# Attention and gated MLP on one core: the first K, Q and V units placed later, their K evictions shared by tokens

## The chip, the core and the metric

The kernel runs on one core of a Trainium2 chip. The core has a matrix engine (TensorE; PE in the profile, with its weight loads as PEld), a vector engine (VectorE, DVE), an activation engine (ScalarE, ACT), a general engine (GpSimd, POOL) and a queue engine (SyncE, SP). Each works through its own instructions in order and waits on semaphores for the others. The metric is the time of one execution on the device, in microseconds; lower is better.

## The reference

x has 2048 tokens of 512 features, all tensors are bfloat16. The result is the sum of three terms:

```
xn  = layernorm(x)
A   = sliding-window attention of xn: 32 heads of 16, causal, window 256; its output @ wo
z   = gelu(x @ w_in)                    # 2048 x 1376, split in z1 and z2, 688 each
z2  = layernorm(z2)
g   = w_sp @ z2 + b_sp                  # w_sp mixes tokens, 2048 x 2048
B   = (z1 * g) @ w_out
out = x + A(xn) + B(xn)
```

Both branches take xn: B's `x` is the normalized x.

## The kernel before

Tokens are cut into 16 blocks of 128. The program has two stages, and the order of every engine's instructions is that of the source (a manual schedule).

**Stage one** (lines 235 to 452) makes everything that needs whole rows first. x arrives by DMA in pairs of blocks. DVE takes mean and variance (`stat_steps`, L316 and L317), blocks 0 to 3 get their root from ACT (`root`, L361) and DVE's reciprocal (`norm_root`, L367), later blocks from a chain of twelve small DVE operations (`rsqrt_steps`, L112 to L129), and `norm_apply` (L321) normalizes in place. `transpose_x` turns a block on PE (L330) and ACT copies it to `xnT` (L333). A *z half* is eight matmuls, one block by one half of w_in (`do_z`, L342); ACT's `gelu` (L358) evicts it to `z1_all` or `z2_all`. z halves have three PSUM buffers. The halves come in a fixed order: both halves of blocks 0 to 8 (`Z_BOTH` is 9), then the second halves of 9 to 15, then the first halves of 9 to 15. `z2_steps` (L208, L214) are DVE's statistics of z2 for its layernorm; one block takes two readings and one aggregation; `z2_norm` (L221) applies them at the end of the stage, for all 16 blocks.

Between z halves stand nine *early units*, the projections that the second stage needs first: K and Q of tokens 0 to 511 for each of four head groups, and V of block 0, in the order K0, Q0, K1, Q1, K2, Q2, K3, Q3, V0 (list `early`). A unit is four matmuls of 512 columns (`unit_k` L157, `unit_q` L176, `unit_v` L191). Their PSUM tiles (`me`) come from the two buffers that the transposes (`tp`) and the first zero matmuls (`wm`) use too, in turn, so a unit waits until the tile two before it has been evicted. A K unit is evicted twice, each time multiplied by one of two head masks (`emask`, e = 0 and 1), into `k_ring`, whose last axes are mask and token: L169 on DVE for e = 0, and for early units L167 on ACT for e = 1. Q is evicted by ACT (L184), V by DVE in four casts of 64 x 256 (L203).

What DVE does around these, in its order: normalization of the last x blocks, `clear_strips` of five attention tiles (ten memsets, L97 and L100), two memsets of ones into `v_ring` (L405), which five transfers of zeros (L270) have filled before, then from block 5 on z2 statistics and evictions in turn. Fourteen matmuls of zeros (L287) keep PE busy while x arrives.

**Stage two** (from line 454) is the attention and the rest of the MLP. 128 gaps `t` each have one `quad` (scores S, L549, exponentials by ACT, L559), masks by DVE (L575), and in between work picked by a budget: further K, Q and V units (PSUM tile `m`, three buffers, tag "w", shared with `gf`), the token mixing `gf` (L473, 512 matmuls, evicted by L479), attention times V (`o_t`, L590) and the outputs (L507, L515). PE's first rows there are S, V1, four gf, S, a Q unit, four gf, S, a second Q unit. V1 is evicted by DVE (L203).

Of the kernel before, what the change touches and what calls it, by code (L numbers as in the profile page):

```python
# [12 lines left out]
ACT = mybir.ActivationFunctionType  # L13
ALU = mybir.AluOpType
# [4 lines left out]
DH = 16  # L19
# [13 lines left out]
HK = 64  # L33
# [5 lines left out]
Z_BOTH = 9  # L39
# [5 lines left out]
def kernel(  # L45
# [12 lines left out]
    nc = tc.nc  # L58
# [13 lines left out]
    k_ring = pers.tile([P, NG, 2 * QRING, 2, HK], BF, name="k_ring")  # L72
    v_ring = pers.tile([P, VRING, 2, H // 2, 2, DH + 1], BF, name="v_ring")
# [3 lines left out]
    emask = pers.tile([P, 2], F32, name="emask")  # L77
# [16 lines left out]
    e_bufs = [ep0.tile([P, 8 * EPAD + HK], BF, name=f"E{i}") for i in range(E_EARLY)]  # L94

    def clear_strips(eb):
        nc.vector.memset(  # L97
            eb[:, 0 : 8 * EPAD].rearrange("p (j c) -> p j c", c=EPAD)[:, :, 0:HK], 0.0
        )
        nc.vector.memset(eb[:, 8 * EPAD : 8 * EPAD + HK], 0.0)  # L100
# [35 lines left out]
    def weave(a, b):  # L136
        for i in range(max(len(a), len(b))):
            if i < len(a):
                a[i]()
            if i < len(b):  # L140
                b[i]()
# [4 lines left out]
    def m_tile(tail=False, early=False):  # L146
        if early:
            return early_pool[0].tile([P, 512], F32, name="me", tag="t")[:]
        if tail:
            t = ps_s.tile([P, 2, 512], F32, name="mt", tag="S")  # L150
            return t[:, 0, :]
        return ps_w.tile([P, 512], F32, name="m", tag="w")[:]

    def unit_k(G, grp, on_act=False, early=False):
        m = m_tile(early=early)
        for c in range(NDC):
            nc.tensor.matmul(  # L157
                m, lhsT=wqkv[:, c, D + G * P : D + (G + 1) * P],
                rhs=xnT[:, 4 * grp : 4 * grp + 4, c, :],
                start=(c == 0), stop=(c == NDC - 1),  # L160
            )
        o = (grp % 2) * 8
        m = m.rearrange("p (a k) -> p a k", k=HK)
        for e in range(2):
            dst = k_ring[:, G, o : o + 8, e, :]
            if on_act and e == 1:
                nc.scalar.activation(out=dst, in_=m, func=ACT.Copy, scale=emask[:, e : e + 1])  # L167
            else:
                nc.vector.tensor_scalar(  # L169
                    out=dst, in0=m, scalar1=emask[:, e : e + 1], scalar2=None, op0=ALU.mult  # L170
                )

    def unit_q(G, grp, on_act=False, early=False):
        m = m_tile(early=early)
# [30 lines left out]
    def z2_steps(n):  # L205
        st = sml.tile([P, 2, nc.vector.BN_STATS_DIM], F32, name="st2")
        steps = [
            lambda j=j: nc.vector.bn_stats(  # L208
                out=st[:, j, :], in_=z2_all[:, n, j * 344 : (j + 1) * 344]
            )  # L210
            for j in range(2)
        ]
        steps.append(
            lambda: nc.vector.bn_aggr(  # L214
                out=mv2[:, n, :], in_=st[:].rearrange("p a b -> p (a b)")
            )
        )
        return steps
# [16 lines left out]
    with tc.tile_pool(name="win_pool", bufs=1) as winp, tc.tile_pool(  # L235
# [8 lines left out]
        nc.vector.memset(esel[:], 1.0)  # L244
        nc.vector.memset(eps_t[:], LN_EPS)
        nc.vector.memset(w_out_sb[:, NFC - 1, :], 0.0)
        early_pool.append(ps_t)
        xs_tiles = {}
        for n2 in range(NB // 2):
# [6 lines left out]
            else:  # L256
                nc.sync.dma_start(
                    out=xs[:],
                    in_=x2[2 * n2 * P : (2 * n2 + 2) * P, :].rearrange("(j p) d -> p j d", p=P),
                )  # L260
            if n2 == 1:
                for c in range(3):
                    (nc.scalar if c < 2 else nc.sync).dma_start(
                        out=w_in_sb[:, c, :], in_=B_w_in[c * P : (c + 1) * P, :]
# [4 lines left out]
        for k in range(VRING):  # L269
            nc.sync.dma_start(  # L270
                out=v_ring[:, k].rearrange("p a g e d -> p (a g e d)").rearrange(
                    "p (r c) -> p r c", c=544
                ),
                in_=warm[:].unsqueeze(1).to_broadcast([P, 2, 544]),
# [5 lines left out]
            out=w_out_sb[:, 0:5, :], in_=B_w_out[0:640, :].rearrange("(c p) n -> p c n", p=P)  # L280
# [2 lines left out]

        make_identity(nc, ident[:])
        wm = ps_t.tile([P, 512], F32, name="wm", tag="t")
        for i in range(14):
            nc.tensor.matmul(wm[:], lhsT=warm[:, 0:P], rhs=warm[:, 0:512], start=True, stop=True)  # L287

        for e in range(2):
            pe = slice(e * HK, (e + 1) * HK)  # L290
            nc.gpsimd.affine_select(
                out=mask2[pe, 0, :], in_=mask2[pe, 0, :], pattern=[[1, HK]],
# [3 lines left out]
                out=mask2[pe, 1, :], in_=mask2[pe, 1, :], pattern=[[-1, HK]],  # L296
# [3 lines left out]
            out=esel[:], in_=esel[:], pattern=[[-32, 4]], compare_op=ALU.is_ge,  # L300
# [3 lines left out]
            out=esel[:], in_=esel[:], pattern=[[32, 4]], compare_op=ALU.is_ge,  # L304
# [7 lines left out]
        def stat_steps(lo, hi):  # L312
            steps = []
            for n in range(lo, hi):
                st = sml.tile([P, nc.vector.BN_STATS_DIM], F32, name="st", bufs=6)
                steps.append(lambda n=n, st=st: nc.vector.bn_stats(out=st[:], in_=xs_tiles[n]))  # L316
                steps.append(lambda n=n, st=st: nc.vector.bn_aggr(out=mvx[:, n, :], in_=st[:]))  # L317
            return steps

        def norm_apply(n):  # L320
            nc.vector.tensor_scalar(  # L321
                out=xs_tiles[n], in0=xs_tiles[n], scalar1=mvx[:, n, 0:1],
                scalar2=rstdx[:, n : n + 1], op0=ALU.subtract, op1=ALU.mult,
            )

        def transpose_x(n):
            tp = ps_t.tile([P, NDC, P], BF, name="tp", tag="t")
            xn = xs_tiles.pop(n)
            for c in range(NDC):
                nc.tensor.transpose(  # L330
                    out=tp[:, c, :], in_=xn[:, c * P : (c + 1) * P], identity=ident[:]
                )
            nc.scalar.copy(out=xnT[:, n], in_=tp[:])  # L333
# [16 lines left out]
        def do_z(n, half):  # L350
            zp = z_tile()
            for c in range(NDC):
                z_part(zp, n, half, c)
            return zp

        def gelu(n, half, zp):
            dst = z1_all if half == 0 else z2_all
            nc.scalar.activation(out=dst[:, n, :], in_=zp[:, 0:FH], func=ACT.Gelu_apprx_tanh)  # L358

        def root(n):  # L360
            nc.scalar.activation(  # L361
                out=rstdx[:, n : n + 1], in_=mvx[:, n, 1:2], func=ACT.Sqrt, bias=eps_t[:],
                scale=1.0,
            )

        def norm_root(n):
            nc.vector.reciprocal(out=rstdx[:, n : n + 1], in_=rstdx[:, n : n + 1])  # L367
            norm_apply(n)
# [5 lines left out]
        root(1)  # L374
        norm_root(0)
        transpose_x(0)
        weave(stat_steps(2, 3), [])
        root(2)
        norm_root(1)
        transpose_x(1)  # L380
        weave(stat_steps(3, 4), [])
        root(3)
        norm_root(2)
# [4 lines left out]
        for lo, hi, nxt in ((4, 8, 8), (8, 12, 14), (12, NB, NB)):  # L388
# [4 lines left out]
            if lo == 4:  # L393
                nc.vector.tensor_reduce(
                    out=emask[:, 0:1], in_=esel[:], op=ALU.add, axis=mybir.AxisListType.X
                )
                nc.vector.tensor_scalar(
                    out=emask[:, 1:2], in0=emask[:, 0:1], scalar1=-1.0, scalar2=1.0,
                    op0=ALU.mult, op1=ALU.add,
                )  # L400
                nc.vector.tensor_copy(out=b_all[:], in_=b_bf[:])
        for eb in e_bufs:
            clear_strips(eb)
        for e in range(2):
            nc.vector.memset(v_ring[e * HK : (e + 1) * HK, :, :, :, e, DH : DH + 1], 1.0)  # L405

        early = [(unit_k, 0), (unit_q, 0), (unit_k, 1), (unit_q, 1), (unit_k, 2), (unit_q, 2),
                 (unit_k, 3), (unit_q, 3), (unit_v, 0)]
        stats_done = 0
# [11 lines left out]
        order = [(1, 1)] + [(n, h) for n in range(2, Z_BOTH) for h in range(2)]  # L421
# [3 lines left out]
        for i, (n, half) in enumerate(order):  # L425
            zp = do_z(n, half)
            if next_t < NB and (half == 0 or n >= Z_BOTH or n == 1):
                transpose_x(next_t)
                next_t += 1
            gelu(n, half, zp)  # L430
            if n >= 6 and (half == 1 or i >= len(order) - 2) and early:
                u, a = early.pop(0)
                if u is unit_v:
                    u(a, early=True)
                else:
                    u(a, 0, on_act=True, early=True)
            if n >= 5:
                ready = n if half == 1 or n < Z_BOTH else NB
                for _ in range(1 if half == 0 and n < Z_BOTH else 2):
                    if stats_done == ready:  # L440
                        break
                    weave(z2_steps(stats_done), [chain.pop(0) for _ in range(3) if chain])
                    stats_done += 1
                    if stats_done == 8:
                        chain += rsqrt_steps(rstd2[:, 0:8], mv2[:, 0:8, 1], 8)
# [221 lines left out]
    for t in range(GAPS):  # L667
        kb, j = divmod(t, 8)
        G, e = divmod(j, 2)
# [46 lines left out]
        while gi < len(g_units) and spent + (C_AV if av else 0) < target:  # L716
            n, hf, c = g_units[gi]
# [50 lines left out]
```

## Time and profile before

| | us |
|---|---|
| median of 3 runs | 306.86 |
| lowest and highest run | 305.71, 307.49 |
| the profiled execution | 305.99 |
| its span, first to last instruction | 304.3 |
| PE busy | 283.2 |
| DVE busy | 194.7 |
| ACT busy | 198.2 |

The span is what the trace covers; the profiled execution's own time is 1.7 us longer. All times of single instructions below count from the span's start. In an order of time, a line has start, duration, engine, source line, operation, what it writes from what it reads, how many were merged, and in brackets how long the engine sat idle before it and what it then waited for. A wait is given as engine and line, then who was waited for: us in total, times, longest. A row of windows gives for each engine its busy time and instructions (PE, PEld, DVE, ACT, POOL), then PE's granted clock (1.00 is full), the share of the DMA engines and GB/s.

### The profile page before, as it was taken

The page shows a single profiled execution, that of the slowest core. Times are in us where ns is not written, and L with a number is a line of the kernel's source. Part 1 is how long each engine was busy: PE and PEld are TensorE (multiplying, and loading weights), DVE is VectorE, ACT ScalarE, POOL GpSimd, SP SyncE. Part 2 cuts the span into 40 slices and gives each one's busy share as a digit, 9 for nine tenths or more (in the row PEclk, how much of TensorE's full clock was granted, in tenths as well). Part 3 has the DMA queues.
Part 4 walks back from the last instruction along what each step waited for, and adds up shares of the span by engine and source line. Part 5 has one row for each costly group of instructions (what it writes and reads, how often), then busy time and mean ns, then how long its engine had stood idle before and what let it go on. Part 6 is the DMA issues. An engine that isn't in the chain of part 4 may idle for free.

```text
span 304.3 us, 7723 instructions
## 1 busy us (share of the span) xinstructions
PE 283.2 (93%) x3186; PEld 163.8 (54%) x3214; DVE 194.7 (64%) x488; ACT 198.2 (65%) x321; POOL 12.0 (4%) x31
## 2 busy tenths in 40 slices
PE   8879269998999999999999999999999999999994
PEld 2546135553545556555655555555555656556761
DVE  4799874699876676646668665876563646453441
ACT  2757047757877777777777767767767777776400
POOL 5000000000000000000000000000000000000000
PEclk9999959999999999999999999999999999999999
DMA  7998200000042508051626124150725144712503
GB/s 252 291 356 188 102 2 1 0 3 0 0 97 52 106 11 148 18 131 39 63 53 147 37 46 88 39 104 11 127 53 119 51 100 89 167 42 63 113 20 96
DMA packets 63842, 26.02 MB, mean 86 GB/s; under 512 B 55696, under 2 KB 62272, under 8 KB 63808
## 3 DMA queue, kind: packets, MB, share of 16 engines
q1 hardware_dynamic: 62560, 22.60, 33.5%
q0 software_dynamic: 816, 2.10, 2.7%
q10 hardware_dynamic: 432, 0.84, 0.8%
q8 instruction: 25, 0.41, 0.6%
q14 instruction: 9, 0.07, 0.1%
HBM read 8.41 MB, written 2.10 MB: 35 GB/s over the span
## 4 chain that ended last, share of the span: by engine, by line
PE 80%; DVE 9%; DMA 5%; ACT 2%; issue 2%; SPq 0%; DVEq 0%
PE gf L473 26%; PE o_t L590 12%; PE S L549 11%; PE m L507 6%; PE zp L342 5%; PE m L191 4%; PE m L515 4%; DMA xs<-in_A_x_dram 4%; PE m L176 4%; PE m L157 4%; DVE st L316 2%; PE me L176 2%; DVE xs L321 1%; DMA oT<-o_norm 1%; DVE st L208 1%
## 5 line engine op out<-in xcount | busy, mean ns | idle before, releaser
L559 ACT ACTIVATE E<-S 128x640 bf16<-128x640 f32 (+4 forms) x256 | 157.5, 667 | 60.2 <-PE S L549 59.9
L473 PE MATMUL gf<-z_all,wspT 128*128 128x344 bf16 x512 | 90.3, 310 | 0.1
L473 PEld LDWEIGHTS <-wspT 128*128 128x128 bf16 x512 | 44.9, 98 | 30.3 <-DMA wspT<-in_B_w_sp_dram 0.3
L590 PEld LDWEIGHTS <-E 128*128 128x128 bf16 x1440 | 45.4, 96 | 10.5 <-DVE E L575 0.6
L575 DVE TENSOR_TENSOR E<-E,mask 128x1024 bf16<-128x1024 bf16 (+1 forms) x64 | 41.6, 651 | 7.7 <-ACT E L559 7.5
L590 PE MATMUL o_t<-v_ring,E 128*128 128x34 bf16 x1440 | 46.0, 177 | 0.0
L549 PE MATMUL S<-q_ring,k_ring 32*128 32x320 bf16 (+4 forms) x576 | 43.9, 280 | 1.7 <-ACT z_all L358 0.8
L342 PE MATMUL zp<-w_in_sb,xnT 128*128 128x512 bf16 (+1 forms) x249 | 41.1, 312 | 0.8 <-DMA w_in_sb<-in_B_w_in_dram 0.4
L479 DVE SCALAR_TENSOR_TENSOR u_sb<-gf,b_all,z_all 128x344 bf16<-128x344 f32 x32 | 18.4, 574 | 24.9 <-PE gf L473 24.8
L342 PEld LDWEIGHTS <-xnT 128*128 128x128 bf16 x256 | 22.7, 99 | 16.8 <-issue 1.9
L549 PEld LDWEIGHTS <-k_ring 32*128 32x128 bf16 x576 | 16.5, 91 | 25.5 <-issue 22.6
L203 DVE CAST v_ring<-m 64x256 bf16<-64x256 f32 x60 | 25.4, 423 | 6.9 <-PE m L191 6.3
L358 ACT ACTIVATE z_all<-zp 128x688 bf16<-128x688 f32 x32 | 23.3, 748 | 6.2 <-PE zp L342 6.2
L519 DVE TENSOR_TENSOR out_sb<-m,x_ch 128x512 bf16<-128x512 f32 x13 | 9.0, 692 | 20.5 <-PE m L515 20.5
L169 DVE TENSOR_SCALAR k_ring<-m,emask 128x512 bf16<-128x512 f32 x24 | 16.9, 745 | 6.7 <-PE m L157 6.6
L495 POOL DMA_DIRECT2D x_ch<-in_A_x_dram x16 | 8.6, 538 | 284.3 <-DVE rsum L606 145.7
L507 PE MATMUL m<-w_out_sb,uT 128*128 128x512 bf16 x67 | 17.3, 380 | 1.2 <-issue 1.0
L333 ACT COPY xnT<-tp 128x512 bf16<-128x512 bf16 x16 | 9.4, 587 | 10.2 <-PE tp L330 10.2
L606 DVE RECIPROCAL rsum<-o_t 128x16 f32<-128x16 f32 x32 | 8.1, 254 | 11.8 <-PE o_t L590 11.7
L191 PE MATMUL m<-wqkv,xnT 128*128 128x512 bf16 x51 | 14.6, 381 | 0.8 <-issue 0.5
L208 DVE BATCH_NORM_STATS2 st<-z_all 128x6 f32<-128x344 bf16 x32 | 14.8, 496 | 0.0
L607 DVE TENSOR_TENSOR o_norm<-o_t,rsum 128x256 bf16<-128x256 f32 x32 | 13.6, 424 | 1.1
(67 smaller groups left out, 177.6 us busy)
## 6 DMA issues: line engine op xcount, KB each, us to landing
x_ch<-in_A_x_dram POOLq DMA_DIRECT2D x16, 128.0 KB, 2.4
out_dram<-out_sb SPq DMA_DIRECT2D x16, 128.0 KB, 1.7
xs<-in_A_x_dram SPq DMA_DIRECT2D x7, 256.0 KB, 8.4
wqkv<-in_A_wqkv_dram SPq DMA_DIRECT2D x1, 1536.0 KB, 11.2
v_ring<-warm SPq DMA_DIRECT2D x5, 272.0 KB, 10.6
w_in_sb<-in_B_w_in_dram ACTq DMA_DIRECT2D x2, 344.0 KB, 5.5
w_in_sb<-in_B_w_in_dram SPq DMA_DIRECT2D x2, 344.0 KB, 7.7
w_out_sb<-in_B_w_out_dram SPq DMA_DIRECT2D x1, 640.0 KB, 5.8
```

The source lines that it names most:

```text
L176: nc.tensor.matmul(m, lhsT=wqkv[:, c, G * P : (G + 1) * P], rhs=xnT[:, 4 * grp : 4 * grp + 4, c, :], start=(c == 0), stop=(c == NDC - 1),)
L191: nc.tensor.matmul(m, lhsT=xnT[:, n, c, :], rhs=wqkv[:, c, 2 * D : 3 * D], start=(c == 0), stop=(c == NDC - 1),)
L203: nc.vector.tensor_copy(out=dst, in_=sr)
L342: nc.tensor.matmul(zp[:, lo:hi], lhsT=xnT[:, n, c, :], rhs=w_in_sb[:, c, f0 + lo : f0 + hi], start=(c == 0), stop=(c == NDC - 1),)
L358: nc.scalar.activation(out=dst[:, n, :], in_=zp[:, 0:FH], func=ACT.Gelu_apprx_tanh)
L473: nc.tensor.matmul(gf[:, 0:GH], lhsT=wsp_tiles[n][:, c, :], rhs=z2_all[:, c, cols], start=(c == 0), stop=(c == NB - 1),)
L479: nc.vector.scalar_tensor_tensor(out=u_sb[:, cols], in0=gf[:, 0:GH], scalar=b_all[:, n : n + 1], in1=z1_all[:, n, cols], op0=ALU.add, op1= ...
L507: nc.tensor.matmul(fo, lhsT=uT[:, c, :], rhs=w_out_sb[:, c, :], start=(c == 0), stop=False)
L549: nc.tensor.matmul(S[:, i, d0 : d0 + w], lhsT=k_ring[32 * s : 32 * s + 32, G, a % (2 * QRING), :, :].rearrange("p e k -> p (e k)"), rhs=q_ ...
L559: nc.scalar.activation(out=data(E, j, j + 2)[:, :, 0:ncol], in_=tiles[pr][:, :, 0:ncol], func=ACT.Exp, scale=SM_SCALE,)
L575: nc.vector.tensor_tensor(out=reg, in0=reg, in1=mk, op=ALU.min)
L590: nc.tensor.matmul(o_t[:, 4 * g2 + s, :, :].rearrange("p e d -> p (e d)"), lhsT=E_tiles[(a // 2, G)][:, base : base + P], rhs=v_ring[:, (a ...
```

## The change

The early units begin at the second half of block 9 (`n >= Z_BOTH`) in place of block 6, one for each z half from there. An early K unit's eviction is split by tokens: DVE takes both masks for the first 256 tokens, ACT both for the last 256. z2 statistics begin at block 8 (`n >= Z_BOTH - 1`) in place of block 5, one or two after each z half. The strips of the five attention tiles are cleared at the very start of DVE's order, and the ones of `v_ring` are written just ahead of V0's eviction. Ten zero matmuls are issued in place of 14, and block 1 is normalized and transposed ahead of the statistics of block 2. Line numbers behind the change move by four to six.

```diff
--- before.py
+++ after.py
@@ -161,14 +161,18 @@
             )
         o = (grp % 2) * 8
         m = m.rearrange("p (a k) -> p a k", k=HK)
-        for e in range(2):
-            dst = k_ring[:, G, o : o + 8, e, :]
-            if on_act and e == 1:
-                nc.scalar.activation(out=dst, in_=m, func=ACT.Copy, scale=emask[:, e : e + 1])
-            else:
-                nc.vector.tensor_scalar(
-                    out=dst, in0=m, scalar1=emask[:, e : e + 1], scalar2=None, op0=ALU.mult
-                )
+        for lo, hi, act in ((0, 4, False), (4, 8, True)) if on_act else ((0, 8, False),):
+            for e in range(2):
+                dst = k_ring[:, G, o + lo : o + hi, e, :]
+                if act:
+                    nc.scalar.activation(
+                        out=dst, in_=m[:, lo:hi, :], func=ACT.Copy, scale=emask[:, e : e + 1]
+                    )
+                else:
+                    nc.vector.tensor_scalar(
+                        out=dst, in0=m[:, lo:hi, :], scalar1=emask[:, e : e + 1], scalar2=None,
+                        op0=ALU.mult,
+                    )
 
     def unit_q(G, grp, on_act=False, early=False):
         m = m_tile(early=early)
@@ -244,6 +248,8 @@
         nc.vector.memset(esel[:], 1.0)
         nc.vector.memset(eps_t[:], LN_EPS)
         nc.vector.memset(w_out_sb[:, NFC - 1, :], 0.0)
+        for eb in e_bufs:
+            clear_strips(eb)
         early_pool.append(ps_t)
         xs_tiles = {}
         for n2 in range(NB // 2):
@@ -283,7 +289,7 @@
 
         make_identity(nc, ident[:])
         wm = ps_t.tile([P, 512], F32, name="wm", tag="t")
-        for i in range(14):
+        for i in range(10):
             nc.tensor.matmul(wm[:], lhsT=warm[:, 0:P], rhs=warm[:, 0:512], start=True, stop=True)
 
         for e in range(2):
@@ -374,10 +380,10 @@
         root(1)
         norm_root(0)
         transpose_x(0)
+        norm_root(1)
+        transpose_x(1)
         weave(stat_steps(2, 3), [])
         root(2)
-        norm_root(1)
-        transpose_x(1)
         weave(stat_steps(3, 4), [])
         root(3)
         norm_root(2)
@@ -399,11 +405,6 @@
                     op0=ALU.mult, op1=ALU.add,
                 )
                 nc.vector.tensor_copy(out=b_all[:], in_=b_bf[:])
-        for eb in e_bufs:
-            clear_strips(eb)
-        for e in range(2):
-            nc.vector.memset(v_ring[e * HK : (e + 1) * HK, :, :, :, e, DH : DH + 1], 1.0)
-
         early = [(unit_k, 0), (unit_q, 0), (unit_k, 1), (unit_q, 1), (unit_k, 2), (unit_q, 2),
                  (unit_k, 3), (unit_q, 3), (unit_v, 0)]
         stats_done = 0
@@ -428,15 +429,20 @@
                 transpose_x(next_t)
                 next_t += 1
             gelu(n, half, zp)
-            if n >= 6 and (half == 1 or i >= len(order) - 2) and early:
+            u = None
+            if n >= Z_BOTH and early:
                 u, a = early.pop(0)
                 if u is unit_v:
+                    for e in range(2):
+                        nc.vector.memset(
+                            v_ring[e * HK : (e + 1) * HK, :, :, :, e, DH : DH + 1], 1.0
+                        )
                     u(a, early=True)
                 else:
                     u(a, 0, on_act=True, early=True)
-            if n >= 5:
+            if n >= Z_BOTH - 1:
                 ready = n if half == 1 or n < Z_BOTH else NB
-                for _ in range(1 if half == 0 and n < Z_BOTH else 2):
+                for _ in range(1 if n < Z_BOTH or u is unit_k else 2):
                     if stats_done == ready:
                         break
                     weave(z2_steps(stats_done), [chain.pop(0) for _ in range(3) if chain])
```

## The prediction

> **What bounds the kernel now.** I read the busy shares and the slices of the span first, then who waited for whom on PE around the hole that the slices show, then the orders of time of PE, DVE and ACT from 27 to 82 us.
>
> The page, parts 1 and 2 (a digit of a slice is a tenth of 7.6 us):
>
> ```profile
> PE 283.2 (93%) x3186; PEld 163.8 (54%) x3214; DVE 194.7 (64%) x488; ACT 198.2 (65%) x321; POOL 12.0 (4%) x31
> PE   8879269998999999999999999999999999999994
> DVE  4799874699876676646668665876563646453441
> PEclk9999959999999999999999999999999999999999
> ```
>
> PE is full from the seventh slice on; ahead of it there is one hole (the fifth slice, digit 2, then one with 6 at half clock), while DVE shows 8 and 7. The waits of PE between 30 and 72 us:
>
> ```profile
> PE me L176 <- ACT k_ring L167: 8.6, 4, 8.1
> ```
>
> So one wait of 8.1 us and three of 0.17. DVE's order of time says why:
>
> ```profile
> 34.88 0.19 DVE L405 MEMSET v_ring<- 64x160 bf16 x1 [0.59 <-issue]
> 35.09 0.94 DVE L208 BATCH_NORM_STATS2 st<-z_all 128x6 f32<-128x344 bf16 x2
> ...
> 39.31 0.70 DVE L169 TENSOR_SCALAR k_ring<-me,emask 128x512 bf16<-128x512 f32 x1
> ...
> 61.26 1.74 DVE L203 CAST v_ring<-me 64x256 bf16<-64x256 f32 x4 [1.58 <-PE me L191]
> ...
> 70.69 3.04 DVE L221 TENSOR_SCALAR z_all<-z_all,mv,rstd 128x688 bf16<-128x688 bf16 x8
> 73.74 1.73 DVE L203 CAST v_ring<-m 64x256 bf16<-64x256 f32 x4
> ```
>
> PE finished the first K unit at 29.94. Its eviction stands in DVE's queue behind x normalization (to 32.04), ten strip clears (to 33.61), the v_ring ones (to 35.09) and four z2 statistics, so it runs at 39.31; ACT's half follows at 40.04, and Q0, which needs that PSUM buffer, starts at 40.78. The windows show the clock's answer:
>
> ```profile
> 37.00:38.00 1.00, 0.00 (x0) 0.00 (x0) 0.97 (x4) 0.00 (x0) 0.00 (x0) 0.73 0.00 0
> 43.00:44.00 1.00, 1.00 (x5) 0.46 (x4) 0.98 (x3) 0.27 (x1) 0.00 (x0) 0.50 0.00 0
> 44.00:45.00 1.00, 1.00 (x10) 0.73 (x9) 0.21 (x1) 0.06 (x1) 0.00 (x0) 0.86 0.00 0
> ```
>
> The third column from the right is granted clock: it halves near 37.5, five us into the hole, and is back near 44.3. Q0 and the z half behind it took 1.86 + 2.04 where other pairs take 1.02 + 1.17: 1.7 us more. From its last matmul at 32.55 to S at 71.39 PE does 16 z halves at 1.166 (two with a transpose fill 25.36 to 27.69), six transposes at 0.22, and eight units at 0.866 (29.08 to 29.94): 26.9 us, in a stretch of 38.8 that ends with 0.83 of entry wait. **Some 11.1 us are hole, slow clock and small waits**; 8.1 and 1.7 are the large ones.
>
> **The change, part by part.**
>
> *Before 27.91 us: nothing.* Ten strip clears (1.57, from 32.04 to 33.61) now stand on DVE between 1.65 and x's landing; DVE waits there 1.80 anyway, until 3.45. Four zero matmuls fewer (4 x 0.43 = 1.7 us) and block 1 normalized before block 2's statistics let z start up to 1.5 us earlier, but its last chunk of w_in lands only at 11.78, and DVE waits until 12.86 for x blocks 6 and 7, which set 16.98 (normalization) and 17.45 (transpose, PE idle 1.67 before it). No transfer moves: what SP, ACT and POOL issue, and in what order, is the same in both builds. If the cover were gone, the strips would cost 1.57 less 1.80, nothing.
>
> *PE up to the new bound.* From 27.91 to the end of K2, PE now does ten z halves (11.66), seven transposes (1.54), and K0, Q0, K1, Q1, K2 (4.33): 45.44. To this come Q0's and Q1's waits for a K unit's buffer. Now a K eviction is DVE 0.75, then ACT 0.69, one after the other: Q starts 1.55 after K ends (46.95 to 48.50), a wait of 0.17. In the changed build's order of waits ACT's first half still waits for DVE's second, so splitting by tokens makes no parallel pair, only four small pieces in place of two. DVE's piece of 128 x 256: bounds are 0.37 (half of 0.745) and 0.745; I take 0.44, the pitch of four 64 x 256 casts in 1.77 (61.26 to 63.03). ACT's: from 0.34 to 0.69, I take 0.43. So 0.88 + 0.85 + 0.08 for two hand-overs = 1.81, 0.42 of wait, twice: **K2 ends at 46.3**.
>
> [...] Were the halves parallel, K2 would end 0.84 earlier.
>
> *The hole goes, DVE is late next.* Statistics begin at block 8, not 5, and only two of the sixteen stand before K0, so DVE idles from about 34 to 36.4. From K2 (46.3) on DVE is never idle in the new order; its sum: K2 0.88, three statistics with three rsqrt steps woven in at 1.19 (52.48 to 53.67) 3.57, K3 0.88, one more 1.19, two plain at 1.04 2.08, v_ring ones 1.48 (33.61 to 35.09 in before; bounds 0.38, their busy time alone, and 1.48; the five v_ring transfers that they wait for were issued by 16.1 and take 10.6, so they are long there), V0's casts 1.77, two statistics 2.08 + 0.1, last rsqrt and sixteen z2 normalizations 7.41 (66.33 to 73.74): 21.4, so 67.7. V1's casts, 1.73 more, end at **69.4**.
>
> *PE meets that.* After K2 it does nine z halves, Q2, K3, Q3, V0 (13.96) and the entry wait 0.83: S starts at 61.1, 10.3 us earlier than 71.39. Then the order is S, V1, gf, S, Q, gf, S and a second Q, which stood at 76.13, 4.74 after S. The three "w" buffers make that Q wait for V1's casts (end 75.47 in before, no wait; the build names them). It is wanted at 65.8, gets its buffer at 69.4: a **new wait of 3.6 us**. It starts 76.13 - 69.4 = **6.7 us earlier**. Behind it on PE stand S, gf and o_t, and ACT's exponentials wait for those S. DVE then lags PE by 0.55 more than in before, just what it had idle at 78.77 (0.56): no further loss. After that everything is the same.
>
> Sum: 11.1 gone, 0.8 spent on the two waits of Q0 and Q1, which leaves 10.3 at S; 3.6 back at the second Q. Span 304.3 - 6.7 = 297.6; the profiled execution took 305.99, so 299.3. Against the median of the runs (306.86) the same gain gives 300.2; I say **299.7**, between the two.
>
> **Rivals.**
>
> A, *no backlog*: DVE's pieces are shorter (ones at 0.38, halves at 0.37), or the second Q gets its buffer in time. For: DVE is only 64% busy. Against: its sum above is 21.4 us in PE's 14.8. If all of it were hidden, 10.3 us gained: 295.7 to 296.5.
>
> B, *the new wait closes the clock gate*, at the second Q, about 66 to 69.4. For: the gate closed once in a wait. Against: that took 4.9 us of stillness, and waits of 1.67 left the clock at 1.00. Price from before: 1.7 us for one half-speed stretch of 3.4 us; gain 5.0: 301 to 302.
> [...]
>
> C, *slower pieces*: 0.745 for DVE's and 0.69 for ACT's. Each costs 0.6 more for K2 and K3 on DVE, and 1.1 at Q0 and Q1: gain 6.7 - 1.2 - 2.3 = 3.2: 303.
>
> D, *slower than before: the gate is not opened by ten zero matmuls*, at z from 11.78 on. In before 14 of them ran at half speed (0.43) to 7.15 and z after them at full (1.17 a half). Left closed, each us of PE work from 11.78 costs another, less the idle 1.67 before 17.45. Past 6.7 + 1.7 = 8.4 us of doubled work, about until 28 us, the gain is gone; closed until K0 (17.3 us, 2.0 of them idle) it is 15.3 - 1.7 = 13.6 lost, 313. Against: after the hole the gate reopened within 3.5 us of dense work, and z is dense.
>
> **Chances.** Forecast (298.2 to 300.9) 0.58; A 0.15; B 0.12; C 0.10; D 0.03; 0.02 for the rest. The range reaches from A to B's and C's near ends: 295.7 to 302.5. Half a per cent is 1.5 us, about what a measurement of this kernel can tell from no change; all cases but D and half of the rest are faster by more, C partly: faster 0.94, same 0.03, slower 0.03.
>
> **What would show it.** No PE wait above 1 us between 30 and 60, clock at 1.00 there; ACT's k_ring pieces start after DVE's second; Q0 and Q1 wait 0.3 to 0.5; DVE without a gap from K2 to V1; S near 61; the second Q of the main loop waits 3 to 4 us on DVE's v_ring cast; the rest of the trace shifted by one amount. Wrong if DVE idles between 47 and 67, if S is later than 63, or if the clock shows 0.50 after 8 us.

## The result, and the profile after

The changed kernel takes 301.77 us (median; 301.71 to 302.49) against 306.40 of the kernel before on the same chip: ratio 0.9851, 95% interval 0.9815 to 0.9887. The profiled execution took 301.71 with a span of 300.0, 4.3 us less than before's 304.3. The forecast was 299.7 in a range of 295.7 to 302.5. In the span, 6.7 us less were forecast and 4.3 came: the hole went and DVE is late next, as forecast, but 2.4 us of the gain are missing.

From the page of the changed kernel, parts 1 and 2:

```profile
PE 284.0 (95%) x3210; PEld 163.0 (54%) x3210; DVE 195.0 (65%) x492; ACT 198.7 (66%) x325; POOL 12.0 (4%) x31
PE   7779989966999999999999999999999999999994
DVE  8699688897875766656658665876744646443441
PEclk9999999997999999999999999999999999999999
```

The hole of the fifth slice is gone. Two new sixes stand in PE's ninth and tenth slice (60 to 75 us), with a 7 of clock in the tenth: the place where stage two begins. Busy PE hardly differs (284.0 and 283.2), so what went is idle time. The waits of PE between 30 and 82 us:

```profile
PE m L180 <- DVE v_ring L207: 3.8, 1, 3.8
PE me L180 <- ACT k_ring L168: 1.0, 2, 0.5
...
```

Before, the longest of this list was one wait of 8.1 us at an early Q unit. Now the longest is the second Q unit of stage two, for a buffer that DVE's V1 casts hold. PE's order of time around it, first the same units in the kernel before, then the changed kernel:

```profile
71.39 0.32 PE L549 MATMUL S<-q_ring,k_ring 32*128 32x320 bf16 x4 [0.83 <-ACT z_all L358]
...
76.13 1.04 PE L176 MATMUL m<-xnT,wqkv 128*128 128x512 bf16 x4
...
79.48 1.04 PE L191 MATMUL m<-wqkv,xnT 128*128 128x512 bf16 x3
```

```profile
61.67 0.32 PE L555 MATMUL S<-q_ring,k_ring 32*128 32x320 bf16 x4 [0.83 <-ACT z_all L364]
...
66.17 0.31 PE L555 MATMUL S<-q_ring,k_ring 32*128 32x320 bf16 x4
70.31 1.59 PE L180 MATMUL m<-xnT,wqkv 128*128 128x512 bf16 x4 [3.83 <-DVE v_ring L207]
...
74.95 1.04 PE L195 MATMUL m<-wqkv,xnT 128*128 128x512 bf16 x4
```

Stage two starts at 61.67 in place of 71.39, 9.7 us earlier. The second Q starts at 70.31 in place of 76.13, 5.8 earlier. The second V unit stands at 74.95 in place of 79.48, 4.5 earlier. So 3.9 us go back in a wait, and another 1.3 in the five us behind it, where the second Q takes 1.59 in place of 1.04. The windows of the same kernel have the reason in the third column from the right, the granted clock:

```profile
70.00:71.00 1.00, 0.69 (x3) 0.34 (x3) 0.85 (x4) 0.00 (x0) 0.00 (x0) 0.81 0.00 0
71.00:72.00 1.00, 1.00 (x5) 0.33 (x3) 1.00 (x3) 0.00 (x0) 0.00 (x0) 0.50 0.00 0
...
74.00:75.00 1.00, 1.00 (x17) 0.66 (x16) 0.53 (x2) 0.47 (x1) 0.00 (x0) 0.98 0.00 0
```

From the second Q to the second V unit, before took 3.35 us and the changed kernel 4.64. In the experiments below it is 3.3 in the three profiled executions that kept a wait for V1's casts and the clock at 1.00, and 4.5 to 4.6 in the four with half clock there.

DVE's order of time shows what it did meanwhile:

```profile
36.57 0.88 DVE L172 TENSOR_SCALAR k_ring<-me,emask 128x256 bf16<-128x256 f32 x2 [2.48 <-PE me L157]
...
46.92 0.88 DVE L172 TENSOR_SCALAR k_ring<-me,emask 128x256 bf16<-128x256 f32 x2 [1.13 <-PE me L157]
...
56.08 0.19 DVE L437 MEMSET v_ring<- 64x160 bf16 x1 [0.59 <-issue]
56.88 0.19 DVE L437 MEMSET v_ring<- 64x160 bf16 x1 [0.60 <-issue]
...
65.46 3.04 DVE L225 TENSOR_SCALAR z_all<-z_all,mv,rstd 128x688 bf16<-128x688 bf16 x8
68.52 1.74 DVE L207 CAST v_ring<-m 64x256 bf16<-64x256 f32 x4
```

It idles 2.48, 1.14 and 1.13 us ahead of K0, K1 and K2, and from K2 (46.92) to the end of V1's casts (70.26) it waits for nobody.

### The profile page after: what moved, and what is told of

It reads as the page before. It is cut to its first block, busy times and chain, and to the rows that moved or that the text cites. A ratio compares the mean times of both kernels' runs of the same rounds, so it can differ in the third digit from the quotient of the medians.

```text
span 300.0 us, 7758 instructions
## 1 busy us (share of the span) xinstructions
PE 284.0 (95%) x3210; PEld 163.0 (54%) x3210; DVE 195.0 (65%) x492; ACT 198.7 (66%) x325; POOL 12.0 (4%) x31
## 4 chain that ended last, share of the span: by engine, by line
PE 80%; DVE 9%; DMA 7%; ACT 1%; issue 1%; SPq 0%; DVEq 0%; ACTq 0%
PE gf L479 25%; PE o_t L596 12%; PE S L555 11%; PE zp L348 6%; PE m L513 6%; PE m L195 5%; PE m L521 4%; DMA xs<-in_A_x_dram 4%; PE m L157 4%; PE m L180 4%; DVE st L212 2%; DVE z_all L225 2%; DMA wspT<-in_B_w_sp_dram 2%; DMA oT<-o_norm 1%; DVE k_ring L172 1%
## 5 line engine op out<-in xcount | busy, mean ns | idle before, releaser
L479 PE MATMUL gf<-z_all,wspT 128*128 128x344 bf16 x512 | 91.3, 313 | 0.1
L555 PEld LDWEIGHTS <-k_ring 32*128 32x128 bf16 x576 | 16.4, 91 | 25.6 <-issue 23.1
L513 PE MATMUL m<-w_out_sb,uT 128*128 128x512 bf16 x78 | 19.1, 381 | 0.0
L180 PE MATMUL m<-xnT,wqkv 128*128 128x512 bf16 x48 | 13.0, 395 | 3.8 <-DVE v_ring L207 3.8
L612 DVE RECIPROCAL rsum<-o_t 128x16 f32<-128x16 f32 x32 | 8.1, 254 | 11.8 <-PE o_t L596 11.7
L195 PE MATMUL m<-wqkv,xnT 128*128 128x512 bf16 x60 | 15.6, 382 | 0.0
```

Of the source, the lines that this page charges most:

```text
L180: nc.tensor.matmul(m, lhsT=wqkv[:, c, G * P : (G + 1) * P], rhs=xnT[:, 4 * grp : 4 * grp + 4, c, :], start=(c == 0), stop=(c == NDC - 1),)
L195: nc.tensor.matmul(m, lhsT=xnT[:, n, c, :], rhs=wqkv[:, c, 2 * D : 3 * D], start=(c == 0), stop=(c == NDC - 1),)
L479: nc.tensor.matmul(gf[:, 0:GH], lhsT=wsp_tiles[n][:, c, :], rhs=z2_all[:, c, cols], start=(c == 0), stop=(c == NB - 1),)
L513: nc.tensor.matmul(fo, lhsT=uT[:, c, :], rhs=w_out_sb[:, c, :], start=(c == 0), stop=False)
L555: nc.tensor.matmul(S[:, i, d0 : d0 + w], lhsT=k_ring[32 * s : 32 * s + 32, G, a % (2 * QRING), :, :].rearrange("p e k -> p (e k)"), rhs=q_ ...
```

## The experiments

**Theory**: the change trades the hole for DVE's lateness; DVE's chain from K2 to V1's casts sets the second Q, and the stillness there halves the clock for a while. **Rivals**: the missing time lies in the split K evictions; or in the start (strips ahead of x, ten zero matmuls); or behind the second Q everything is late anyway, so that the wait itself matters little. Each ratio is to the kernel before on the same chip, whose medians are 305.72 to 306.64 on the chips used; the changed kernel is at 301.8 (0.985). Differences of medians between chips carry some tenths of a us; distances within a trace don't.

### The ones back to their old place

```diff
+        for e in range(2):
+            nc.vector.memset(v_ring[e * HK : (e + 1) * HK, :, :, :, e, DH : DH + 1], 1.0)
         early = [(unit_k, 0), (unit_q, 0), ...
...
                 if u is unit_v:
-                    for e in range(2):
-                        nc.vector.memset(v_ring[...], 1.0)
                     u(a, early=True)
```

> The ones of v_ring go back to their old place behind x normalization; the rest is the changed kernel. Theory (the second Q unit of stage two waits for V1's casts at the end of DVE's chain, and the half clock after that wait costs 1.3 us): DVE idles 2.48 us before K0, which takes the 1.5 us of the ones, so V1's casts end 1.6 us earlier, the wait of 3.83 us becomes about 2.2, too short to close the clock; 1.6 + 1.3 = 2.9 us less than 301.8, so 298.9. Rival 1 (the missing 2.4 us lie in the split K evictions and their waits for Q0 and Q1): no change, 301.8. Rival 2 (the clock falls whatever the length of the wait): 300.2.

Measured: 299.74, ratio 0.9774 (0.9753 to 0.9794): 2.0 us less. PE's waits of this kernel, 5 to 82 us:

```profile
PE m L180 <- DVE v_ring L207: 2.1, 1, 2.1
PE tp L336 <- DVE xs L327: 2.0, 1, 2.0
PE me L180 <- ACT k_ring L168: 1.0, 2, 0.5
...
```

The wait is 2.1, as the theory had it (2.2), and in the profiled execution the clock behind it is 1.00. Rival 1 is out: the waits for the split evictions are the same 1.0 and the time fell (what the split costs is measured below). That the time is 0.8 above the forecast has one cause visible in the profiled execution: there the clock fell to 0.50 after another wait, that of 1.99 us for x at 16.5, and cost 1.7 us (last section).

For the other executions the record has the mean granted clock over the span. A half-clock stretch of 3.4 us in 300 lowers it by 0.006. A fall behind PE's last matmul, which costs nothing, lowers it by 0.001 to 0.003 (0.999 with the early statistics and 0.997 with eight extra matmuls, whose traces show that fall and no other). So 0.994 or less tells of a stretch at half clock, 0.997 or more of none that matters. All four executions here have 0.992 to 0.994: each had one, and its place is known for the profiled one alone. So the time doesn't exclude rival 2 (300.2); that the shorter wait spares the clock rests on one trace. That 2.2 us are too short to close it was an estimate, from waits of up to 1.67 us in the kernel before, behind which the clock stayed at 1.00.

### Extra matmuls in the wait, eight and fourteen

```diff
+        if t == 1:
+            dm = ps_o.tile([P, 512], F32, name="dm", tag="o")
+            for _ in range(8):
+                nc.tensor.matmul(
+                    dm[:], lhsT=xnT[:, 0, 0, :], rhs=wqkv[:, 0, 0:512], start=True, stop=True
+                )
         if av:
```

> The changed kernel with eight extra matmuls of 512 columns (results unused) on PE just behind the gf matmuls and the S of the second gap, where PE waits for the buffer of the second Q. Theory: they fill 1.7 of the 3.83 us of the wait, the clock stays at 1.00 behind it, the second Q starts at the same 70.3 us, and the 1.3 us of half clock are gone: 300.5. Rival (what is lost behind the second Q is DVE's lag, not the clock): 301.8 or more.

Measured: 301.75, ratio 0.9842 (0.9812 to 0.9873), executions from 300.48 to 303.51: no gain that stands out. The trace shows the theory's part: the rest of the wait is 2.1, the clock 1.00, the second Q takes 1.02 and the second V unit stands at 73.88, 11.97 us behind S, where the changed kernel takes 13.28. But the profiled span is 299.9, for this execution lost 1.1 us near 256 us to something else:

```profile
PE m L180 <- DVE v_ring L207: 2.1, 1, 2.1
PE gf L479 <- DMA wspT<-in_B_w_sp_dram: 1.1, 1, 1.1
...
```

The six executions come in two groups: 300.48, 300.85 and 301.60 with a mean clock of 0.997 to 1.000, and 301.90, 303.10 and 303.51 with 0.988 to 0.992. So with 2.1 us of the wait left the clock still fell somewhere in half of the executions; where it didn't, the two that were not profiled are near the theory's 300.5. As a measurement of the clock's price the median is inconclusive. It was made once more with fourteen (3.0 of 3.8 us), beside the changed kernel itself on one chip:

> The changed kernel with 14 extra matmuls (results unused) in the wait, 3.0 us of 3.8, so that less than a us of stillness is left. Theory (half clock costs 1.3 us): clock 1.00 throughout, second Q at the same 70.3 us and full speed, 1.3 us less than the changed kernel beside it. Rival (the clock behind the wait costs nothing that the rest doesn't give back): no difference, within 0.5 us.

> The changed kernel once more, beside the next two on one chip. Theory: second Q waits 3.8 us on V1's casts, clock at 0.50 for 3.4 us behind or inside the wait, 301.8 within 0.5. If the place of the half clock moves from run to run, the second Q's own time (1.59 us before, 1.02 at full clock) moves with it.

Measured: 300.75, ratio 0.9829 (0.9808 to 0.9850), with fourteen; 301.79, ratio 0.9857 (0.9838 to 0.9877), for the changed kernel beside it. The executions are 299.97 to 301.33 and 301.32 to 303.29: 1.0 us between the medians, though the two intervals overlap. The mean clock is 0.997 to 1.000 in the four with fourteen and 0.986 to 0.996 in the five of the changed kernel. The second Q and the second V unit in the two traces, with fourteen and without:

```profile
69.33 1.02 PE L180 MATMUL m<-xnT,wqkv 128*128 128x512 bf16 x4 [0.80 <-DVE v_ring L207]
...
72.67 1.04 PE L195 MATMUL m<-wqkv,xnT 128*128 128x512 bf16 x4
```

```profile
71.10 1.56 PE L180 MATMUL m<-xnT,wqkv 128*128 128x512 bf16 x4 [3.83 <-DVE v_ring L207]
...
75.74 1.04 PE L195 MATMUL m<-wqkv,xnT 128*128 128x512 bf16 x4
```

From one to the other go 3.34 us and 4.64: 1.3. So the clock's share is 1.3 in the trace, and about 1 in the time. In both the second Q stands 8.6 us behind S, as in the changed kernel and with eight: DVE's chain sets it, whatever PE does in the wait. The repeated changed kernel kept its wait (3.83) and its half clock.

### The old K eviction

```diff
-        for lo, hi, act in ((0, 4, False), (4, 8, True)) if on_act else ((0, 8, False),):
-            for e in range(2):
-                dst = k_ring[:, G, o + lo : o + hi, e, :]
...
+        for e in range(2):
+            dst = k_ring[:, G, o : o + 8, e, :]
+            if on_act and e == 1:
+                nc.scalar.activation(out=dst, in_=m, func=ACT.Copy, scale=emask[:, e : e + 1])
...
```

> The changed kernel with the old K eviction (DVE all tokens with mask 0, then ACT all tokens with mask 1). Theory (the two engines take turns at one PSUM buffer anyway, so four pieces only add fixed cost): Q0 and Q1 wait 0.17 us each in place of 0.51, DVE spends 0.75 in place of 0.88 on a K unit, V1's casts end 0.9 to 1.0 us earlier, so 300.9, or 299.5 if the shorter wait also spares the clock. Rival (the split makes the evictions shorter): Q0 and Q1 wait longer than 0.51, 302.3 or more.

Measured: 300.87, ratio 0.9805 (0.9781 to 0.9828), 0.9 less than the changed kernel. PE's waits, 30 to 82 us:

```profile
PE m L176 <- DVE v_ring L203: 3.6, 1, 3.6
...
PE me L176 <- ACT k_ring L167: 0.3, 2, 0.2
```

The two waits for a K unit fall from 1.0 to 0.3 together, the long wait stays. The four executions spread over 1.6 us and one of them has a mean clock of 1.000, so the medians alone would not carry 0.9; the traces do: from the transpose of block 4, which waits for x, to the second V unit go 56.65 us here and 57.58 in the changed kernel. Splitting by tokens cost time, because DVE and ACT still read one PSUM buffer in turn: in the changed kernel ACT waited for DVE's second piece in all four units (0.61, 0.60, 0.60 and 1.40 us), and a K unit took 0.88 on DVE and 0.84 on ACT in place of 0.75 and 0.69. The first of the four on ACT (DVE began at 36.57):

```profile
37.54 0.84 ACT L168 ACTIVATE k_ring<-me,emask 128x256 bf16<-128x256 f32 x2 [0.61 <-DVE k_ring L172]
```

### Statistics earlier

```diff
-            if n >= Z_BOTH - 1:
+            if n >= Z_BOTH - 2:
                 ready = n if half == 1 or n < Z_BOTH else NB
-                for _ in range(1 if n < Z_BOTH or u is unit_k else 2):
+                for _ in range(1 if n < Z_BOTH else 2):
```

> The changed kernel with z2 statistics from block 7 on, and two after each z half from block 9 on: 4, 4 and 4 ahead of K0, K1 and K2 in place of 2, 3 and 3. Theory: they fill 4.75 us in which DVE idled before K0, K1 and K2; DVE ends V1's casts near 66.7, the second Q wants its buffer at 66.5, so the wait falls from 3.83 to under 0.5 and the clock stays at 1.00: 4.9 us less, 296.9. Rival (DVE has no room there, so that K evictions come later by as much): K2 one to two us later, S later, 300 or more.

Measured: 297.12, ratio 0.9702 (0.9673 to 0.9731), forecast 296.9. The list of PE's waits from 30 to 82 us has no v_ring any more:

```profile
PE me L180 <- ACT k_ring L168: 1.0, 2, 0.5
PE S L555 <- ACT z_all L364: 0.8, 1, 0.8
PE S L555 <- ACT E L565: 0.5, 2, 0.3
```

Nothing was taken away: the same sixteen statistics stand where DVE idled. With the old K eviction as well:

> The changed kernel with both: statistics from block 7 on, two after each z half from block 9 on, and the old K eviction. Theory: what is left on PE after the early statistics are the waits of Q0 and Q1; they fall from 0.51 to 0.17 each, 0.7 less than the 297.1 of the early statistics alone: 296.4. Rival (DVE is still late there): 297.1 or more.

Measured: **295.89**, ratio 0.9669 (0.9643 to 0.9695), the fastest version here, 3.3% under the kernel before and 5.9 us under the changed one; the rival (297.1 or more) is out.

### V1's casts on ACT

```diff
-        misc.append((n * 8, ready, unit_v, (n,)))
+        misc.append((n * 8, ready, unit_v, (n, n == 1)))
```

> The changed kernel with one edit: V1's four casts go to ACT, which waits for PE there, and no longer stand behind sixteen normalizations on DVE. Theory (the second Q waits for V1's buffer and nothing else that is late): the second Q starts near 67.5 (S waits about a us for ACT), the wait of 3.8 us and the half clock are gone, the next V unit stands about 3.7 us earlier, 298.2. Rival (gf and o_t need what DVE ends at 68.5 to 70 just as much, so the wait only moves to them): 300.5 or more.

Measured: 297.35, ratio 0.9728 (0.9707 to 0.9750), forecast 298.2. The second Q stands 5.7 us behind S (60.81 to 66.51), in place of 8.6, with S waiting 0.3 for ACT twice. The rival fails: gf and o_t did not inherit the wait. One buffer held by one late eviction was most of it: from S to the second V unit go 9.13 us, against 13.28 in the changed kernel and 8.09 before.

### One part of the change alone

```diff
-            if n >= 6 and (half == 1 or i >= len(order) - 2) and early:
+            u = None
+            if n >= Z_BOTH and early:
...
-            if n >= 5:
+            if n >= Z_BOTH - 1:
                 ready = n if half == 1 or n < Z_BOTH else NB
-                for _ in range(1 if half == 0 and n < Z_BOTH else 2):
+                for _ in range(1 if n < Z_BOTH or u is unit_k else 2):
```

> The kernel before with one part of the change alone: early units from block 9 on, z2 statistics from block 8 on. Strips and ones stay behind x normalization, K evictions are not split, 14 zero matmuls. Theory: this part alone removes the hole; strips, ones and two statistics end near 37.2, 0.6 us after K0, so Q0 waits about 0.85 us and Q1 0.17; the ones are out of the chain behind K2, V1's casts end near 68.3, the second Q waits about 2.2 us and the clock stays at 1.00 behind it: 7.8 us less than 306.6, 298.8, less than the whole change takes (301.8). Rival (the strips ahead of x and the split carry part of the gain): 302 or more.

Measured: 298.53, ratio 0.9747 (0.9722 to 0.9772), forecast 298.8: **the later units and statistics alone gain 7.9 us, more than the whole change (4.6)**. The other parts together cost 3.2; two of them, measured above, make 2.0 (the ones) and 0.9 (the split). The waits came near the forecast (0.7 for 0.85 at Q0, 1.85 for 2.2 at the second Q), the clock did not: in the profiled execution it fell after the wait of 1.85 us, see the last section. The mean clock is 0.993 or 0.994 in three of the six executions (298.33 to 299.41) and 0.999 or 1.000 in the other three (297.44 to 298.80): one kernel, the same waits, and the clock falls in about every second execution.

```diff
         early_pool.append(ps_t)
...
+        for eb in e_bufs:
+            clear_strips(eb)
...
-        for eb in e_bufs:
-            clear_strips(eb)
```

> The kernel before with one part alone: the five strips cleared ahead of x. Theory: DVE reaches the first K eviction 1.57 us earlier, the hole shrinks from 8.1 to 6.5 us, the clock still halves: 1.6 us less, 305.0. Rival (they delay x at the start): 306.6 or more.

Measured: 305.22, ratio 0.9957 (0.9934 to 0.9979): 1.2 us less. The longest wait at an early Q fell from 8.1 to 6.5 as forecast.

```diff
-        for i in range(10):
+        for i in range(14):
...
-        norm_root(1)
-        transpose_x(1)
         weave(stat_steps(2, 3), [])
         root(2)
+        norm_root(1)
+        transpose_x(1)
```

> The changed kernel with 14 zero matmuls and block 1 normalized behind block 2's statistics, as before. Theory (the start is bound by the transfers of w_in and x): no difference, 301.8, within half a us. Rival (ten leave the clock closed for a while, or save time at the start): a us or more either way.

Measured: 301.86, ratio 0.9861 (0.9833 to 0.9888): no difference. The last chunk of w_in still starts its matmuls at 11.84 (11.83 in the changed kernel).

## Why the prediction was right, and what was mis-sized

- *The number*: 301.77 lies outside the 298.2 to 300.9 to which the forecast itself gave 0.58, and in rival B's 301 to 302. The range held it because it took in the near ends of B and C; that part is luck.
- *Bound and hole*: right. Block 6's K0 behind DVE's backlog was the hole; moved to block 9 it is gone, and the part alone gains 7.9 us.
- *Before 27.91 us nothing changes*: right, by the run with fourteen zero matmuls (301.86); with the strips ahead of x, DVE's first statistics start at 3.49 in place of 3.45.
- *ACT still waits for DVE's second piece, so the split makes no pair*: right. In before ACT had sat idle 11.8 us in its four waits on DVE's K eviction, 10.0 of them at K0; with the split it waits 3.2 us in four, and DVE and ACT still follow one another. The split costs more than I put: 0.9 us by the run without it and its trace.
- *K2 ends at 46.3*: **mis-sized**. Q0 and Q1 cost PE 0.68 each, not 0.42: a wait of 0.51, and ahead of it a transpose of 0.39 that takes 0.22 where the next matmul follows at once. I took the start of PE's next matmul for the end of the K unit; the eviction starts 0.2 us after that (36.37 and 36.57). With the same 0.2 once more ahead of K2, DVE began on K2 at 46.92, not 46.3.
- *DVE's sum from K2 to the end of V1's casts, 23.1*: measured 23.34 (46.92 to 70.26). The ones took 1.6 (1.48 put). The two terms together put the second Q at 70.31, not 69.4, and its wait at 3.83, not 3.6: 0.9 us of the missing 2.4.
- *No further loss behind the second Q*: **this step failed**. The clock fell at 70.6 and stayed at 0.50 until 74.0, which cost 1.3 us, so the rest of the trace did not shift by one amount (5.8 at the second Q, 4.5 at the second V unit). The ground that I gave, DVE's lag, held: with the clock at 1.00 and fourteen extra matmuls the second V unit follows the second Q by 3.34 us, as before (3.35). The clock was there as rival B, with a chance of 0.12 and a price of 1.7. Its half-speed stretch of 3.4 us was an estimate: before shows one stretch of 6.8 us (37.4 to 44.3), 3.5 of them with PE at work. Where I said that stillness of 4.9 us had been needed, I had read one wait of 8 us as a threshold. In the repeat the clock fell there again (71.4), and 1.85 us were enough in the run with one part alone.
- The last 0.2 us (4.5 at the second V unit, 4.3 at the end) lie at 256 us, where the weight load of gf waits 0.50 us for wspT in the changed kernel and 0.26 before. In seven of the other profiled executions PE itself waits there, 0.5 to 1.1 us. No experiment was made on it; its cause stays open.
- *Rival A* did not come: DVE's pieces were no shorter than put. But the DVE that is late is the DVE that idled 4.75 us ahead of K0 to K2. The forecast noted that idling ahead of K0 and did not ask whether it could be filled; two changed lines do it (297.12), and with the old eviction the kernel is 5.9 us faster.

## What to carry to other kernels

Moving work behind a hole also moves what stood in the hole: sum the other engine's in-order chain up to the next buffer that the bound engine needs, and look whether that engine idles just before the chain. Splitting an eviction between two engines that read one PSUM buffer in turn gained nothing here: 0.88 and 0.84 us in place of 0.75 and 0.69, and the kernel without it is 0.9 us faster. Price a wait on TensorE with the half clock that may follow (here 1.3 us behind a wait of 3.83), and test each part of a change alone: here one part was worth more than the whole (7.9 us against 4.6).

## What the runs showed of the hardware

**The clock fell in or behind waits of 1.85 us and more, and not at each of them.** The kernel with the later units alone, its windows around the second Q:

```profile
66.00:67.00 1.00, 0.00 (x0) 0.00 (x0) 0.97 (x3) 0.70 (x2) 0.00 (x0) 1.00 0.00 0
67.00:68.00 1.00, 0.78 (x3) 0.34 (x3) 0.85 (x4) 0.00 (x0) 0.00 (x0) 0.69 0.00 0
68.00:69.00 1.00, 1.00 (x4) 0.34 (x3) 0.92 (x3) 0.00 (x0) 0.00 (x0) 0.50 0.00 0
...
70.00:71.00 1.00, 1.00 (x8) 0.53 (x5) 0.00 (x0) 0.77 (x2) 0.00 (x0) 0.60 0.00 0
```

PE was still for 1.85 us (65.4 to 67.2), and the clock halved at 67.4, when PE was at work again, for 3.4 us. A wait of 2.10 at the same place, in the profiled execution of the kernel with the ones back, left it at 1.00. The changed kernel, run again, at its start, where PE waits for x:

```profile
16.48 0.40 PE L336 MATMUL tp<-ident,xs 128*128 128x128 bf16 x4 [2.06 <-DVE xs L327]
16.71 4.17 PE L348 MATMUL zp<-w_in_sb,xnT 128*128 128x512 bf16 x16
...
20.95 2.50 PE L348 MATMUL zp<-w_in_sb,xnT 128*128 128x512 bf16 x16
```

The same sixteen matmuls take 4.17 and then 2.50: here 2.06 us were enough. Of the waits of 1.99 us at that place, the one in the kernel with the ones back closed the clock (again 4.17 us for the sixteen), those in the fastest version and in the kernel with the later units alone did not (2.50). So the length of the wait alone does not decide. Ahead of PE's last matmul, each low stretch that the windows show whole lasted 3.4 us or, behind the hole of 8.1 us, 6.8; behind the hole of 6.5 the clock was at 0.50 from 36.0 or earlier to 41.2. Each fall that they show began 2.0 to 4.8 us after PE had stopped.

In the 3.4 us ahead of the fall at 67.4, as long as the low stretch behind it, PE stood still for 1.85 and worked for the rest. What decides whether a wait closes the clock, and when, was not shown.

**The wait for x ends at a different time in each execution.** The transpose of block 4, which waits for x by way of DVE's normalization, starts between 16.4 and 17.9 us in the thirteen profiled executions, and at 17.4 and 16.5 in two of one kernel, the changed one. A span compared from one profile each therefore carries about a us; distances within a trace (S to the second Q) don't.
